# Decoding 64-bit weights: the sign by an 8-bit conversion, or by a parametric ReLU and a shift

## The chip, the cores and the metric

The kernel runs on one core of a Trainium2 chip. The metric is the device time of one execution in microseconds (us). Before the change it is 1642.6 us, the median of three runs (1642.33 to 1644.14).

The core has five engines with queues of their own, and each takes its instructions strictly in the order in which they were queued: PE (TensorE: matmuls and transposes), DVE (VectorE), ACT (ScalarE), POOL (GpSimd) and SP (SyncE, which here only issues DMAs). An instruction that waits holds up everything behind it on its engine, and nothing on the others until they need its result.

## The reference

Two blocks follow each other: an attention that keeps the 32 largest scores of each row, and a two-layer network with an ELU between the layers.

```python
# q, k, v: (8, 8, 576, 64) float32
scores = scale * np.matmul(q, k.transpose(0, 1, 3, 2))
kth = np.partition(scores, -32, axis=-1)[..., -32:-31]
scores = np.where(scores >= kth, scores, -1e9)
attn = softmax(scores)                        # with + 1e-9 in the denominator
x = np.matmul(attn, v)                        # -> (4608, 512), float32

# w_in (512, 2048), w_out (2048, 512): float64
h = x @ w_in
g = np.where(h > 0, h, np.exp(np.minimum(h, 0)) - 1)
out = (g @ w_out).astype(np.float32)
```

What matters here is that the two weight matrices arrive as float64. No engine computes in that type, so the kernel makes float32 words out of the 64-bit words itself. That is the *decoding*.

## The kernel before, in words

**Attention.** There are 144 *steps*. A step handles one tile of query rows and one pair of heads: two *rows* of 128 x 576 scores. For each row DVE runs four `MAX8` and three `MATCH_REPLACE8` (lines 350, 354 and 360 in the first eight steps, 373, 378 and 385 after them) to find the 32nd largest score. ACT copies the scores out of PSUM (L339), masks them (L407) and takes the exponential (L408). POOL normalises (`normalise`, L418 to L425: a chain that begins with the tile `dene` and ends with two multiplications of `sc`). PE transposes the result (L444), ACT copies it out (L445), PE multiplies it with V (L470), and ACT copies that into `xT` (L497). The masks of a step come one step or more after its `MAX8`s, and `normalise` one step after the masks.

**Network.** When the `xT` of a block of tokens is full, its matmuls go into a list: the hidden layer (L545), the ELU around it (L555 to L564 on ACT, L515 on POOL or L517 on DVE), and the projection (L573). `feed` takes pieces from this list between the passes of a step, by a budget that is reckoned when the program is written out; it is the same before and after the change.

**Decoding.** The weights are cut into 32 *pieces* of 128 x 512 numbers, 16 of `w_in` and 16 of `w_out`. Each is loaded as 128 x 1024 32-bit words (`load_weight`, L155, issued on SP) into one of eight `raw` buffers, and goes through four stages, every one on strided words (each second one):

1. `convert_first`, on POOL (L176): the high words, read as float32, are clamped. Below this is called the *clamp*.
2. `convert_second`, on ACT (L182, L183, L185): this function is what changes.
3. `convert_third`, on DVE (L189): the words that stage 2 left in the place of the low words are shifted left by 3.
4. `convert_last`, on POOL (L193): those are added as integers to the words that stage 2 left in the weight tile. Below this is called the *add*. It frees the `raw` buffer, and so lets the load of the piece eight places later be issued.

`decode_piece(i)` issues the load of piece i + 3, the clamp of piece i, stage 2 of piece i - 1, stage 3 of i - 3 and stage 4 of i - 4. `hook` calls it twice in each row of the first seven steps, and after that three times in a step. So in the order in which the program is written, the add of a piece comes right behind the clamp of the piece four later.

**Who sets the order.** From the ninth step on (`n == tight`, with `tight` = 8) the order on each engine is the written one (`manual_schedule`, L729). The first eight steps, in which most of the decoding lies, are outside it, and there the framework itself orders each engine's instructions when the program is made. The profile shows where it left the written order. When the last piece is done, the buffers of the decoding are given up, and others take their place, among them those into which the K and Q of the second batch are loaded (`load_halves`, L231).

Of the kernel before, what the change touches and what calls it, by code (L numbers as in the profile page):

```python
# [8 lines left out]
AF = mybir.ActivationFunctionType  # L9
ALU = mybir.AluOpType  # L10
FP32 = mybir.dt.float32
U32 = mybir.dt.uint32
I32 = mybir.dt.int32
FP8 = mybir.dt.float8e4
PSUM = bass.MemoryType.PSUM

TOP_K = 32
# [64 lines left out]
def kernel(  # L82
# [9 lines left out]
    nc = tc.nc  # L92
# [15 lines left out]
    scale = 1.0 / float(D) ** 0.5  # L108
# [35 lines left out]
    def weight(i):  # L144
        per = dff // WN
        if i < NC * per:
            f, c = divmod(i, NC)
            src = moe_w_in[c * P : (c + 1) * P, 2 * f * WN : 2 * (f + 1) * WN]
            return src, w_in[:, c, f * WN : (f + 1) * WN]
        f = i - NC * per  # L150
        return moe_w_out[f * P : (f + 1) * P, :], w_out[:, f, :]
# [6 lines left out]
    def parts(t):  # L158
        words = t[:].rearrange("p (n w) -> p n w", w=2)
        return words[:, :, 0], words[:, :, 1]  # L160
# [16 lines left out]

    def convert_second(i):
        lo, hi = parts(raw[i])
        ef = hi.bitcast(FP32)  # L180
        w = weight(i)[1]
        nc.scalar.activation(w, lo, AF.Copy, scale=2.0**-35, bias=2.0**17)  # L182
        nc.scalar.activation(lo.bitcast(FP32), ef, AF.Abs, scale=2.0**-112)  # L183
        signs = w.bitcast(FP8).rearrange("p (n w) -> p n w", w=4)[:, :, 3]
        nc.scalar.activation(signs, ef, AF.Copy, scale=2.0**-30, saturate=False)  # L185

    def convert_third(i):
        lo = parts(raw[i])[0]
# [22 lines left out]
    def decode_piece(i):  # L211
        if i + 3 < 2 * NF:
            load_weight(i + 3)
        apart = 1 if i >= scheduled else 0
        stages = [(0, convert_first), (1, convert_second)]
        if i != scheduled:
            stages += [(3 + apart, convert_third), (4 + apart, convert_last)]
        for ago, stage in stages:
            if 0 <= i - ago < 2 * NF:
                stage(i - ago)  # L220
        decoded[0] = max(0, i - 3 - apart)
# [380 lines left out]
    for b in range(B):  # L602
# [28 lines left out]
        for qts in order:  # L631
# [3 lines left out]
            for qt in qts:  # L635
                n = len(steps)
# [155 lines left out]
```

## Time and profile before

| | |
|---|---|
| median of three runs | 1642.6 us (1642.33 to 1644.14) |
| span of the profiled execution, first to last instruction | 1640.8 us |
| median less this span | 1.8 us |
| busy: PE, DVE, ACT, POOL | 1581.7, 1453.4, 1187.7, 708.7 us |
| first and last instruction of the decoding | 3.1 us (load), 153.7 us (last add ends) |

The profile names an execution's span only; its time outside the span isn't shown, and the 1.8 us above stand in for it. Every number of the profile comes from one execution. "Idle before" is the time in which an engine stood still just before an instruction, and behind "<-" stands who ended that wait. A clock below 1.00 for PE ("PEclk") means that PE was granted that share of its full speed, and its matmuls take longer in proportion.

### The profile page before, as it was taken

The page shows a single profiled execution, that of the slowest core. Times are in us where ns is not written, and L with a number is a line of the kernel's source. Part 1 is how long each engine was busy: PE and PEld are TensorE (multiplying, and loading weights), DVE is VectorE, ACT ScalarE, POOL GpSimd, SP SyncE. Part 2 cuts the span into 40 slices and gives each one's busy share as a digit, 9 for nine tenths or more (in the row PEclk, how much of TensorE's full clock was granted, in tenths as well). Part 3 has the DMA queues.
Part 4 walks back from the last instruction along what each step waited for, and adds up shares of the span by engine and source line. Part 5 has one row for each costly group of instructions (what it writes and reads, how often), then busy time and mean ns, then how long its engine had stood idle before and what let it go on. Part 6 is the DMA issues. An engine that isn't in the chain of part 4 may idle for free.

```text
span 1640.8 us, 25344 instructions
## 1 busy us (share of the span) xinstructions
PE 1581.7 (96%) x8276; PEld 1011.8 (62%) x8276; DVE 1453.4 (89%) x2981; ACT 1187.7 (72%) x2400; POOL 708.7 (43%) x1534
## 2 busy tenths in 40 slices
PE   4788999999999999999999999999999999999999
PEld 3566777666575757555566666655557575755564
DVE  6987999999999999999999699999999599998000
ACT  6887778778695867778678686868759595958521
POOL 4775445445353534445335353535435353534300
PEclk8579999999999999999999999999999999999999
DMA  7431221012100310012100211012100201000000
GB/s 226 151 128 25 50 40 26 7 22 45 42 1 7 59 42 8 7 22 44 36 14 15 43 30 28 1 28 44 36 14 0 43 1 35 1 13 2 7 13 14
DMA packets 188037, 56.18 MB, mean 34 GB/s; under 512 B 178177, under 2 KB 179201, under 8 KB 187905
## 3 DMA queue, kind: packets, MB, share of 16 engines
q1 hardware_dynamic: 186704, 54.26, 14.1%
q8 instruction: 66, 1.08, 0.3%
q14 instruction: 67, 0.54, 0.1%
q10 hardware_dynamic: 1200, 0.30, 0.1%
HBM read 45.09 MB, written 9.44 MB: 33 GB/s over the span
## 4 chain that ended last, share of the span: by engine, by line
PE 76%; ACT 12%; DVE 7%; POOL 3%; issue 1%; DMA 1%; SPq 0%; ACTq 0%; DVEq 0%; POOLq 0%
PE ops L573 29%; PE hps L545 23%; PE avps L470 10%; PE scps L331 7%; PE eps L444 6%; DVE wk L378 3%; DVE m L385 3%; ACT sc L408 2%; ACT et L445 2%; ACT sc L407 2%; DVE m L373 1%; ACT n L564 1%; ACT n L555 1%; ACT sc L339 1%; ACT n L560 1%
## 5 line engine op out<-in xcount | busy, mean ns | idle before, releaser
L385 DVE MAX8 m<-wk 128x8 f32<-128x576 f32 x816 | 577.9, 752 | 0.3 <-POOL den L406 0.3
L545 PE MATMUL hps<-xT,w_in 128*128 128x256 f32 (+2 forms) x2432 | 545.8, 374 | 0.0
L573 PE MATMUL ops<-w_out,gT 128*128 128x512 f32 x1152 | 523.6, 599 | 0.0
L545 PEld LDWEIGHTS hps<-xT,w_in 128*128 128x128 f32 x2432 | 406.0, 192 | 100.1 <-issue 26.3
L378 DVE MATCH_REPLACE8 wk<-m,wk 128x576 f32<-128x576 f32 x544 | 401.4, 748 | 0.0
L573 PEld LDWEIGHTS ops<-w_out,gT 128*128 128x128 f32 x1152 | 209.0, 190 | 233.9 <-issue 232.8
L418 POOL TENSOR_SCALAR dene<-den 128x2 f32<-128x2 f32 x144 | 32.9, 228 | 686.5 <-ACT sc L408 686.1
L408 ACT ACTIVATE sc<-sc,den 128x576 f32<-128x576 f32 x288 | 223.6, 776 | 65.5 <-POOL den L406 44.2
L407 ACT ACTIVATE sc<-sc,m 128x576 f32<-128x576 f32 x288 | 225.3, 782 | 10.8 <-DVE m L385 10.7
L470 PE MATMUL avps<-et,vT 128*64 128x256 f32 (+2 forms) x2080 | 207.2, 330 | 17.4 <-ACT et L445 17.2
L425 POOL TENSOR_SCALAR sc<-sc,rec 128x576 f32<-128x576 f32 x288 | 213.0, 750 | 15.0 <-POOL rec L423 0.2
L331 PE MATMUL scps<-kqT 64*128 64x288 f32 (+1 forms) x1280 | 206.0, 442 | 13.6 <-ACT kqT L307 9.1
L339 ACT ACTIVATE sc<-scps 128x576 f32<-128x576 f32 x288 | 171.8, 647 | 65.1 <-PE scps L331 65.1
L445 ACT COPY et<-eps 128x512 f32<-128x512 f32 x288 | 164.6, 571 | 73.4 <-PE eps L444 73.4
L378 DVE MATCH_REPLACE8 wk<-m,sc 128x576 f32<-128x576 f32 x272 | 200.6, 748 | 0.0
L373 DVE MAX8 m<-sc 128x8 f32<-128x576 f32 x272 | 191.6, 749 | 8.8 <-ACT sc L339 8.8
L444 PEld LDWEIGHTS eps<-ident,sc 128*128 128x128 f32 x1152 | 144.9, 144 | 87.2 <-issue 52.7
L444 PE MATMUL eps<-ident,sc 128*128 128x128 f32 x1152 | 177.1, 279 | 13.7 <-POOL sc L425 13.7
L470 PEld LDWEIGHTS avps<-et,vT 128*64 128x64 f32 x2080 | 128.5, 142 | 98.8 <-ACT et L445 31.7
L515 POOL TENSOR_TENSOR gT<-n,gT 128x512 f32<-128x512 f32 (+1 forms) x119 | 164.9, 1386 | 31.2 <-ACT n L564 31.1
L331 PEld LDWEIGHTS scps<-kqT 64*128 64x128 f32 (+1 forms) x1280 | 111.3, 182 | 89.5 <-issue 43.8
L555 ACT ACTIVATE n<-hps 128x512 f32<-128x512 f32 (+1 forms) x156 | 87.3, 559 | 56.8 <-PE hps L545 56.0
(53 smaller groups left out, 1089.6 us busy)
## 6 DMA issues: line engine op xcount, KB each, us to landing
raw<-in_moe_w_in_dram SPq DMA_DIRECT2D x16, 512.0 KB, 6.1
vT<-in_v_dram SPq DMA_DIRECT2D x64, 128.0 KB, 2.5
raw<-in_moe_w_out_dram SPq DMA_DIRECT2D x16, 512.0 KB, 3.6
out_dram<-osb SPq DMA_DIRECT2D x32, 256.0 KB, 2.1
kin<-in_k_dram SPq DMA_DIRECT2D x112, 72.0 KB, 2.5
qin<-in_q_dram SPq DMA_DIRECT2D x112, 72.0 KB, 2.6
kin<-in_k_dram SPq DMA_DIRECT2D x8, 128.0 KB, 4.5
vT<-in_v_dram SPq DMA_DIRECT2D x64, 16.0 KB, 2.2
```

The lines of the kernel that those rows point to most:

```text
L331: nc.tensor.matmul(wide[i][rows, half, 0:HS], kq[part, q0 : q0 + u.t.ql], kq[part, k0 : k0 + HS], start=True, stop=True,)
L373: nc.vector.max(found[i], cur[i])
L378: nc.vector.match_replace(wk[i], found[i], cur[i], TAKEN)
L385: nc.vector.max(found[i], cur[i])
L407: nc.scalar.activation(sc, sc, AF.Prelu, scale=-1.0, bias=low, alpha=1.0 / STEEP)
L408: nc.scalar.activation(sc, sc, AF.Exp, scale=-STEEP, bias=gap, accum_out=u.den[:, i : i + 1])
L425: nc.gpsimd.tensor_scalar(u.sc[:, i, :], u.sc[:, i, :], rec[:, i : i + 1], 1.0, ALU.mult, ALU.mult)
L444: nc.tensor.transpose(ps[:, c * P : (c + 1) * P], sc[:, c0 : c0 + P], ident[:])
L445: nc.scalar.copy(g.et[:, chunks, u.at, :], ps[:, 0 : n * P].rearrange("p (c q) -> p c q", c=n),)
L470: nc.tensor.matmul(ps[i * D : (i + 1) * D, cols], vt[:, 2 * J + i if c == J else i * J + c, :], w, start=(c == 0), stop=(c == J),)
L545: nc.tensor.matmul(blk.h[:, f % bank, :], w_in[:, i, f * P : (f + 1) * P], blk.xT[:, i, 0:n_tok], start=(i == 0), stop=(i == NC - 1),)
L573: nc.tensor.matmul(blk.o[:], blk.gT[f // NG][:, f % NG, s * P : (s + 1) * P], w_out[:, f, :], start=(f == 0), stop=(f == NF - 1),)
```

## The change

Only `convert_second` changes. Before, ACT runs three instructions for each piece. The first writes the low words, scaled, as float32 with an offset of 2^17, so that the rounded low word sits in the last bits of that number. The second takes the absolute value of the high words, scaled, and writes it over the low words. The third writes the sign of each high word as an 8-bit float into the top byte of the weight word, and by that also clears the bits that the offset had left there.

After, it runs two. The first writes the scaled low words as rounded 32-bit integers, so there is nothing to clear. The second is a parametric ReLU over the high words: positive ones are scaled by 2^-112 as before, negative ones by a further 2^32, which sets a bit that the left shift of stage 3 moves into the place of the sign, while the sign bit itself is shifted out. Clamp, shift and add are unchanged.

```diff
-FP8 = mybir.dt.float8e4
...
     def convert_second(i):
         lo, hi = parts(raw[i])
-        ef = hi.bitcast(FP32)
-        w = weight(i)[1]
-        nc.scalar.activation(w, lo, AF.Copy, scale=2.0**-35, bias=2.0**17)
-        nc.scalar.activation(lo.bitcast(FP32), ef, AF.Abs, scale=2.0**-112)
-        signs = w.bitcast(FP8).rearrange("p (n w) -> p n w", w=4)[:, :, 3]
-        nc.scalar.activation(signs, ef, AF.Copy, scale=2.0**-30, saturate=False)
+        w = weight(i)[1].bitcast(I32)
+        nc.scalar.activation(w, lo, AF.Copy, scale=2.0**-29)
+        nc.scalar.activation(
+            lo.bitcast(FP32), hi.bitcast(FP32), AF.Prelu,
+            scale=2.0**-112, alpha=2.0**32,
+        )
```

## The prediction

> **What bounds the kernel now.** I read the busy table by stage first. The decoding lies in the first 154 us, so I cut there, and at the point from which the chain that ended last runs through PE alone.
>
> ```profile
> core 0: us, PE busy (x) PEld busy (x) DVE busy (x) ACT busy (x) POOL busy (x), PEclk, DMA share, GB/s
> 0.00:47.00 47.00, 26.10 (x111) 18.00 (x112) 32.39 (x69) 32.57 (x67) 20.95 (x40) 0.84 0.77 229
> 47.00:112.00 65.00, 52.72 (x252) 38.13 (x250) 58.52 (x117) 56.31 (x116) 45.44 (x64) 0.62 0.43 130
> 112.00:162.00 50.00, 42.92 (x224) 29.55 (x226) 40.30 (x80) 41.15 (x85) 30.74 (x53) 0.83 0.17 46
> 162.00:318.00 156.00, 152.88 (x1213) 112.91 (x1210) 154.48 (x319) 121.34 (x248) 69.54 (x163) 1.00 0.17 33
> 318.00:1640.00 1322.00, 1307.12 (x6483) 813.22 (x6483) 1167.69 (x2399) 936.35 (x1887) 541.99 (x1217) 1.00 0.11 22
> ```
>
> From 162 us on, PE or DVE is full: DVE stands still for 1.5 of 156 us, later PE for 15 of 1322. Nothing of the decoding is left there and the order is the written one, so that part can only start earlier or later as a whole. Before 162 us no engine is full: PE stands still for 40 us, DVE for 31, ACT for 32. Whatever the change is worth is decided there, and then kept to the end.
>
> Second, the waits between 47 and 112 us (time in all, times, longest).
>
> ```profile
> POOL raw L176 <- DMA raw<-in_moe_w_out_dram: 14.3, 7, 2.4
> ...
> PE eps L444 <- POOL sc L425: 10.7, 4, 4.3
> ACT et L445 <- PE eps L444: 8.6, 3, 3.2
> DVE raw L189 <- ACT raw L183: 4.2, 2, 2.5
> ...
> POOL raw L176 <- DMA raw<-in_moe_w_in_dram: 2.2, 1, 2.2
> ```
>
> The largest is POOL's clamp waiting for a weight to land. PE and ACT then wait for POOL. ACT itself holds up DVE for 4.2 us only. The timeline of POOL shows one round of this.
>
> ```profile
> 77.64 1.29 POOL L193 TENSOR_TENSOR w_in<-w_in,raw 128x512 int32<-128x512 int32 x1
> ...
> 84.02 1.28 POOL L176 TENSOR_SCALAR raw<-raw 128x512 f32<-128x512 f32 x2
> 85.25 1.29 POOL L193 TENSOR_TENSOR w_in<-w_in,raw 128x512 int32<-128x512 int32 x1
> 86.49 1.29 POOL L193 TENSOR_TENSOR w_out<-w_out,raw 128x512 int32<-128x512 int32 x1
> 90.14 0.66 POOL L176 TENSOR_SCALAR raw<-raw 128x512 f32<-128x512 f32 x1 [2.36 <-DMA raw<-in_moe_w_out_dram]
> 92.37 0.66 POOL L176 TENSOR_SCALAR raw<-raw 128x512 f32<-128x512 f32 x1 [1.57 <-DMA raw<-in_moe_w_out_dram]
> 92.98 2.56 POOL L193 TENSOR_TENSOR w_out<-w_out,raw 128x512 int32<-128x512 int32 x2
> ```
>
> Counting the L193s and L176s from the start, the two at 85.25 and 86.49 are the adds of pieces 15 and 16, those at 90.14 and 92.37 the clamps of 23 and 24. Piece 24 is loaded into the buffer that add 16 frees at 87.8, lands 4.6 us later, and POOL, which takes its queue in order, has stood still meanwhile with the adds of 17 and 18 behind it. As written, add 17 comes right behind clamp 21, but the queue has it behind clamp 24. So POOL runs in a ring: two adds 2.7 us, normalising 3.5, two clamps 1.3, two adds 2.5, the load 4.6, a clamp 0.6, together 15.2; from the adds at 77.64 to those at 92.98 it is 15.3. DVE's selection with its four shifts needs 11 us a step (14 passes at 0.66 from start to start, six value loads at 0.07, four shifts at 0.33), ACT 12.5 (four pieces at 1.76 and 5.5 for the rest), POOL without the wait 11.
>
> Why are the adds late? ACT runs behind: the masks at 90 us are those of row 9, while DVE searches row 12. Stage 2 of a piece comes late by as much, so shift and add do too. Between 47 and 112 us ACT is busy for 56 of 65 us, and its costliest part there is what the change touches:
>
> ```profile
> L183 ACT ACTIVATE raw<-raw 128x512 f32<-128x512 f32 x18 | 12.3, 683 | 0.0
> L185 ACT ACTIVATE w_out<-raw 128x512 fp8e4<-128x512 f32 x9 | 7.3, 807 | 0.0
> L185 ACT ACTIVATE w_in<-raw 128x512 fp8e4<-128x512 f32 x9 | 7.1, 784 | 0.0
> ...
> L407 ACT ACTIVATE sc<-sc,m 128x576 f32<-128x576 f32 x8 | 6.3, 784 | 0.0
> ...
> L182 ACT ACTIVATE w_in<-raw 128x512 f32<-128x512 uint32 x9 | 5.8, 679 | 0.0
> ```
>
> **The change part by part.** *The sign instruction goes.* 32 times 0.787 us are 25.2 us busy; from its start to the next start it is 0.64 us, so ACT gets 20.5 us of queue back, 2.6 in a step of four pieces (12.5 becomes 10). Where does this lie on the path?
>
> Up to 47 us the chain of waits runs through ACT at 33.6 to 38.0 and 39.8 to 42.7, with three sign instructions in it: 3 x 0.64 = 1.9 us, on the path. Between 47 and 112 the ring has no ACT step in it. If POOL's queue kept its order, ACT would only wait longer, and the gain there would be nothing. But these steps lie outside the hand-written order, and the lag of the adds, seven places instead of four, comes from ACT being the fullest engine. With ACT at 10 and DVE at 11, the reason for the lag is gone, and I expect the adds one or more places earlier against the clamps. Each place is one clamp and one add, 1.9 us, by which the load starts earlier; two places cover most of the 4.6 us. The wait at stake is 14.3 + 2.2 = 16.5 us. The end can't take all of it, because DVE is not held up that much: in this stretch it stands still for 6.5 us and its shifts take 587 instead of their usual 428 ns (17 x 0.16 = 2.7). So DVE's part is between 0 and 9 us. I take 5, a little over half, since an order that is made anew seldom removes every wait.
>
> From 112 to 162 us DVE stands still for 10 us, 4.4 of them for an ELU at 121 to 126 us while ACT works off its lag without a gap, and 5.7 for one at 157 to 162 that waits for PE's hidden layer. The first goes with the lag; for the second PE is late, and its 7 us of standing still in this stretch, in front of transposes that wait for POOL and ACT, shrink with it in part. The chain there holds two sign instructions at 141 to 148 us (1.3 us). Bounds 1.3 and 10; I take 3.5.
>
> *Parametric ReLU for the absolute value.* The trace has no such instruction on strided words. Bounds: L183 itself at 0.68 us, and the ReLU of the mask (L407), at 0.78 for 576 elements with a column as bias. That makes 0 to 0.1 us each, at most 3.2 us of ACT. I take 0, as the operands are those of L183, and 0.5 on the path as the far end.
>
> *Integers for floats as output.* L182 takes 0.68 us with float output. The nearest row with another output type is L185 at 0.79, so 0 to 0.11 each, below 3.5 us on ACT; a gain is excluded, as element count and strides stay. I take 0: both outputs are four bytes wide, L185 writes single bytes.
>
> *Waits.* The shift waited for L183, second of the three, and now waits for the ReLU, which is last of two: the same position. The add waited for the sign too, but POOL stood still for it only at the first two pieces (3.2 us at 11 and 15 us, where DVE has no score to search yet), so I count nothing. POOL and SP get no new instructions; SP's loads come when the adds do, and behind them the K and Q loads of the second batch, which wait for the last add (32.6 us in the waits of SP). They move with it.
>
> One page of the Trainium skill speaks against the change. "ScalarE: Activation LUTs", in "What ACT_TABLE_LOAD costs", says that a function outside the active table set costs a reload of about 2.66 us, and its list of sets doesn't name parametric ReLU; at two reloads a piece that would be 170 us. The row decides: the whole execution shows one table load of 1.28 us, at 2.8 us, though L407 (parametric ReLU) and L408 (exponential) alternate 288 times. So no reload enters the sum.
>
> Sum: 1.9 + 5 + 3.5 = 10.4, less 0.5 for the ReLU, about 10 us. The span goes from 1640.8 to 1631; with the 1.8 us outside it, which I leave as they are, 1632.7, or 9.9 under the median of 1642.6.
>
> **The rivals.** A measurement of this kernel can tell about 0.2%, 3.3 us, from no change.
>
> *The ring stays* (0.17). POOL keeps its order, and only 1.9 + 1.3 = 3.2 us on ACT's own path go: 1639.4, just at the bound. For it: the ring holds no ACT instruction. Against it: the lag of the adds does come from ACT.
>
> *Everything closes up* (0.14). The 16.2 us in which DVE stands still between 16 and 162 us, and 4.4 of its stretched shifts (32 x 0.14), all go: up to 20 us, 1622. Against it: PE and DVE depend on each other at 112 to 162 us, where PE's clock is 0.83 and PE is 86% busy.
>
> *The new order is worse: slower* (0.19). Today one of the two loads of a round is hidden under the normalising (3.5 us) and the clamps. If the new order puts normalising elsewhere, or a clamp in front of the pair of adds that frees its buffer's successor, the second load is laid open too, about 4 us a round, in five rounds up to 20 us; I take half, 1652. It decides as soon as less than 4.6 us of other POOL work stands between an add and the clamp eight places on. For it: the order is made from expected durations, and it has already put clamps too early once. Against it: less work on ACT brings adds forward, not back.
>
> *The new instructions cost more than the old* (below 0.03): at their upper bounds 3.2 + 3.5 = 6.7 us of ACT against 20.5 saved. The profile excludes a loss by this alone.
>
> **How the numbers follow.** Forecast 1632.7 with chance 0.50; by the bounds of its terms its own range is 1626 to 1638. The ring's case is divided by the bound, and a piece of the slower case lies within it. Faster by over 0.2%: 0.50 + 0.14 + 0.02 = 0.66. Within 0.2%: 0.16. Slower: 0.18. The range from 1622 to 1649 leaves out a piece of the closing case (0.05) and the far part of the slower one (0.10).
>
> **What would show it.** Right: L185 gone; the first two lines at 0.65 to 0.75 us; one table load; between 47 and 112 us POOL's wait for weights well under 16.5 us, with the add of a piece five or six clamps behind instead of seven; DVE's first `MAX8` of the ninth step (L373) before 106 us instead of 110.4; from 162 us on the same busy times, shifted. Wrong: the wait for weights as large as before, at an end less than 5 us earlier; or a second wait for weights in each round, and a later end; or the gain at 112 us there and given back by 318, which would mean that PE, not DVE, was late.

## The result, and the profile after

| | before | after |
|---|---|---|
| median | 1642.5 us (1639.8 to 1644.1, 4 runs) | 1634.2 us (1633.5 to 1634.5, 4 runs) |
| ratio | | 0.9945, 95% interval 0.9931 to 0.9959 |
| span of the profiled execution | 1640.8 us | 1632.6 us |
| busy: ACT, DVE | 1187.7, 1453.4 us | 1168.2, 1451.1 us |

The forecast was 1632.7 us. The time came out 1.5 us above it and the span fell by 8.2 us where 10 were forecast. In the changed kernel the line numbers behind L176 are lower by one: the clamp is L175, stage 2 is L180 and L181, the shift L188, the add L192.

First the busy table by stage, cut at the same times as before (length; busy time of PE, its weight loads, DVE, ACT and POOL; granted clock, DMA share, GB/s).

```profile
0.00:47.00 47.00, 28.80 (x113) 19.36 (x113) 32.53 (x69) 29.55 (x64) 21.31 (x41) 0.85 0.79 232
47.00:112.00 65.00, 52.11 (x250) 38.70 (x251) 54.67 (x110) 50.97 (x110) 52.34 (x73) 0.67 0.46 145
112.00:162.00 50.00, 46.04 (x298) 32.69 (x299) 49.08 (x102) 36.29 (x75) 23.73 (x43) 0.96 0.18 37
162.00:318.00 156.00, 150.99 (x1174) 110.08 (x1172) 154.88 (x320) 121.61 (x250) 70.98 (x167) 1.00 0.15 29
```

From 162 us on nothing but the start has moved. Up to that point ACT is busy for 13.2 us less. DVE did *less* than before between 47 and 112 us (54.7 for 58.5 us) and is then full: 49.1 of 50 us, for 40.3 before.

Second, the groups of ACT's instructions up to 162 us. Both new lines cost what the old ones did, and there is one table load.

```profile
L181 ACT ACTIVATE raw<-raw 128x512 f32<-128x512 f32 x32 | 20.5, 678 | 0.6 <-POOL raw L175 0.2
...
L180 ACT ACTIVATE w_out<-raw 128x512 int32<-128x512 uint32 x16 | 10.3, 682 | 0.0
...
L180 ACT ACT_TABLE_LOAD x1 | 1.3, 1283 | 2.8 <-issue 2.8
```

Third, the waits between 47 and 112 us.

```profile
PE eps L443 <- POOL sc L424: 13.8, 5, 4.0
ACT et L444 <- PE eps L443: 10.4, 5, 4.1
POOL raw L175 <- DMA raw<-in_moe_w_out_dram: 9.8, 6, 3.3
DVE raw L188 <- ACT raw L181: 6.2, 6, 3.1
```

POOL's wait for weights is 9.8 us for 14.3 + 2.2 before. Fourth, POOL's timeline shows why.

```profile
64.07 0.66 POOL L175 TENSOR_SCALAR raw<-raw 128x512 f32<-128x512 f32 x1
64.69 1.29 POOL L192 TENSOR_TENSOR w_in<-w_in,raw 128x512 int32<-128x512 int32 x1
65.95 0.66 POOL L175 TENSOR_SCALAR raw<-raw 128x512 f32<-128x512 f32 x1
66.55 1.31 POOL L192 TENSOR_TENSOR w_in<-w_in,raw 128x512 int32<-128x512 int32 x1
69.62 0.66 POOL L175 TENSOR_SCALAR raw<-raw 128x512 f32<-128x512 f32 x1 [1.76 <-DMA raw<-in_moe_w_out_dram]
```

Clamp and add now alternate instead of coming in pairs, and from the tenth add on the add of a piece stands behind the clamp five or six places later (six and seven by turns before); only the 22nd still has seven. Compared instruction by instruction, ACT's queue is the one of before with the sign instructions taken out and nothing else moved. The queues of POOL, DVE, SP and PE were ordered differently.

So the forecast's picture seems to hold: the ring was loosened, and the time fell. Whether the one caused the other is what the experiments ask, since three things happened together: the sign instructions went, POOL's order changed, and so did DVE's (with a few places on SP and PE).

### The profile page after: what moved, and what is told of

Read it like the earlier page. It is cut to its first block, busy times and chain, and to the rows that moved or that the text cites. A ratio compares the mean times of both kernels' runs of the same rounds, so it can differ in the third digit from the quotient of the medians.

```text
span 1632.6 us, 25282 instructions
## 1 busy us (share of the span) xinstructions
PE 1579.2 (97%) x8276; PEld 1009.8 (62%) x8276; DVE 1451.1 (89%) x2981; ACT 1168.2 (72%) x2368; POOL 708.9 (43%) x1534
## 4 chain that ended last, share of the span: by engine, by line
PE 74%; DVE 11%; ACT 9%; POOL 3%; issue 1%; DMA 1%; SPq 0%; ACTq 0%; DVEq 0%; POOLq 0%
PE ops L572 28%; PE hps L544 23%; PE avps L469 9%; PE scps L330 7%; PE eps L443 6%; DVE wk L377 4%; DVE m L384 3%; ACT sc L407 2%; ACT sc L406 1%; ACT et L444 1%; DVE m L372 1%; DVE wk L353 1%; ACT n L563 1%; DVE m L359 1%; DMA raw<-in_moe_w_out_dram 1%
## 5 line engine op out<-in xcount | busy, mean ns | idle before, releaser
L469 PE MATMUL avps<-et,vT 128*64 128x256 f32 (+2 forms) x2080 | 204.4, 327 | 14.3 <-ACT et L444 14.1
L443 PE MATMUL eps<-ident,sc 128*128 128x128 f32 x1152 | 176.6, 279 | 13.8 <-POOL sc L424 13.8
L330 PEld LDWEIGHTS scps<-kqT 64*128 64x128 f32 (+1 forms) x1280 | 111.0, 183 | 86.4 <-issue 45.5
```

The costliest lines, as they stand in the source:

```text
L330: nc.tensor.matmul(wide[i][rows, half, 0:HS], kq[part, q0 : q0 + u.t.ql], kq[part, k0 : k0 + HS], start=True, stop=True,)
L443: nc.tensor.transpose(ps[:, c * P : (c + 1) * P], sc[:, c0 : c0 + P], ident[:])
L469: nc.tensor.matmul(ps[i * D : (i + 1) * D, cols], vt[:, 2 * J + i if c == J else i * J + c, :], w, start=(c == 0), stop=(c == J),)
```

## The experiments

All of them are variations of the two kernels in those first eight steps. For each, POOL's idle time just ahead of clamps behind 47 us was summed from its timeline ("POOL waits"), and three points in time were read from the timelines: the start of the 20th and of the 32nd add, and the end of the masks of the sixth step (ACT's last L408 of that step). All are us. A ratio is against runs of the kernel before on the same chip, so it can differ from the ratio of the medians by some 0.06%; gains are worked out from ratios below unless two medians are named.

| kernel | median us | ratio, 95% interval | POOL waits | 20th add | sixth masks | 32nd add |
|---|---|---|---|---|---|---|
| before | 1642.5 | 1 | 17.1 | 100.9 | 108.5 | 152.4 |
| int_fp8 | 1642.9 | 1.0001, 0.9989 to 1.0014 | 15.6 | 100.6 | 108.4 | 152.1 |
| b_pin7 | 1638.7 | 0.9982, 0.9969 to 0.9995 | 10.2 | 96.2 | 106.0 | 150.0 |
| b_pin6 | 1636.0 | 0.9966, 0.9954 to 0.9978 | 0 | 94.2 | 103.2 | 148.8 |
| a_ccaa | 1635.6 | 0.9956, 0.9941 to 0.9972 | 12.7 | 101.9 | 102.2 | 148.1 |
| a_old | 1634.6 | 0.9957, 0.9945 to 0.9969 | 14.9 | 100.9 | 100.4 | 146.7 |
| after | 1634.2 | 0.9945, 0.9931 to 0.9959 | 9.8 | 93.1 | 101.5 | 147.0 |
| a_pin6 | 1632.9 | 0.9938, 0.9924 to 0.9952 | 0.5 | 88.8 | 96.8 | 143.4 |
| a_pin5 | 1632.8 | 0.9941, 0.9929 to 0.9954 | 0 | 88.2 | 96.7 | 143.4 |
| b_written | 1651.6 | 1.0061, 1.0049 to 1.0073 | 0 | 104.1 | 112.9 | 163.4 |
| a_written | 1640.3 | 0.9993, 0.9984 to 1.0003 | 0 | 96.2 | 101.2 | 153.2 |

The kernels whose name begins with b have the three instructions of before in stage 2, those with a the two of after. Outside the written pair, the first also have DVE's order of before, the second that of after; no run has the two instructions with DVE's old order.

**int_fp8: integers as output, and nothing else.** The first instruction of before writes integers; the absolute value and the sign stay.

```diff
-        nc.scalar.activation(w, lo, AF.Copy, scale=2.0**-35, bias=2.0**17)
+        nc.scalar.activation(w.bitcast(I32), lo, AF.Copy, scale=2.0**-29)
```

> One half of the change alone: the low words as rounded integers, the sign still by the third ACT instruction; as planned, every engine's queue is the one of before. Theory (POOL's queue order and the ring of loads carry the gain): the same as before, 1640.5 to 1644.5 us, POOL's wait for weights at 47 to 112 us about 16 us. Rival 1 (the integer output itself is cheaper or dearer on ACT): the first line's mean moves by 0.05 us or more from 0.68, and the time by 2 us or more. Rival 2 (ACT's freed queue time carries the gain): also the same as before.

Measured 1642.9 us, no difference. All queues were those of before. The group of this line in its profile:

```profile
L182 ACT ACTIVATE w_out<-raw 128x512 int32<-128x512 uint32 x16 | 10.3, 680 | 0.0
```

So rounding to integers is free, as the forecast took it. The kernel also serves as a repeat of before: with the same order, POOL's wait came out at 15.6 instead of 17.1 us.

**b_pin7: before, with the ring loosened a little.** Each clamp is queued behind the add of the piece seven earlier. Nothing is taken from ACT, and the queues of PE, DVE and ACT are those of before.

```diff
-        nc.gpsimd.tensor_scalar(ef, ef, top, -top, ALU.min, ALU.max)
+        clamp = nc.gpsimd.tensor_scalar(ef, ef, top, -top, ALU.min, ALU.max)
+        if i - 7 in adds:
+            tc.add_manual_dep(clamp.ins, adds[i - 7].name, ...)
...
-        nc.gpsimd.tensor_tensor(w, w, parts(t)[0].bitcast(I32), ALU.add)
+        adds[i] = nc.gpsimd.tensor_tensor(...).ins
```

> The kernel before with all its ACT work, but on POOL each clamp is queued behind the add of the piece seven places earlier, so that adds and clamps alternate as they do after the change; the queues of PE, DVE, ACT and SP are those of before. Theory (POOL's order carries the gain): most of it appears without the change, 1634 to 1638 us, with POOL's wait for weights at 47 to 112 us near 10 us. Rival (ACT's freed queue time carries it): 1641 to 1644 us.

Measured 1638.7 us: 3 us of gain, between the two expectations.

**a_ccaa: after, with POOL's pairs brought back.** From the tenth add on, POOL takes two clamps and then two adds, the add of each odd piece behind the clamp seven places on. For that `decode_piece` also writes adds and loads in pairs, which moves a few places in SP's queue.

```diff
+        if 9 <= i <= 22:
+            tc.add_manual_dep(add, made[i + 7 if i % 2 else 1 - i].name, ...)
...
```

> The changed kernel with two ACT instructions a piece, but on POOL two clamps and two adds by turns, with the adds six and seven clamps behind as before the change; the queues of PE, DVE and ACT are those of after. Theory (POOL's order): most of the gain goes, 1638 to 1643 us, with a wait for weights of 13 to 18 us at 47 to 112 us. Rival (ACT's freed queue time): 1632 to 1636 us.

Measured 1635.6 us, although POOL's wait is back at 12.7 us. That went against the order of clamps and adds as the cause.

**a_pin6: after, with the ring loosened fully.** The edit of b_pin7 with six in the place of seven, on the changed kernel.

> The changed kernel, with each clamp queued behind the add of the piece six places earlier, so that the adds are one place nearer than after; only POOL's queue differs from after. Theory (POOL's order): the rest of the wait for weights, 9.8 us at 47 to 112 us, falls below 4 us, and the time to 1627 to 1632 us. Rival (ACT): 1632 to 1636 us. Third case (PE or DVE is late next): the wait falls and the time stays at 1632 to 1636 us.

Measured 1632.9 us. POOL's wait for weights is gone (0.5 us), and the end moves by little: 1.3 us between these medians, 2.8 when both kernels were measured on one chip (below).

**a_old: after, with the whole sequence of clamps and adds of before.** A table gives for every add the clamp that it follows, so that POOL takes clamps and adds in the order that it had before; only the 24th add comes one clamp earlier than it did. ACT's and DVE's queues are those of after, PE's and SP's differ in a few places (`decode_piece` writes loads in pairs here too). Where normalising stands between them is left to the framework, and it put it earlier.

```diff
+LAG = {4: 2, 5: 3, 6: 3, 7: 6, 8: 6, 23: 6}
+LAG.update((j, 7 if j % 2 else 6) for j in range(9, 23))
...
+        for late in (clamps.get(i + LAG.get(i, 0)), adds.get(i - 1)):
+            if late is not None and 4 <= i <= 23:
+                tc.add_manual_dep(add, late.name, ...)
...
```

> The changed kernel with clamps and adds on POOL in exactly the sequence of before, from the fifth add to the 24th (the run with two clamps and two adds by turns kept the changed sequence up to the ninth add); DVE's and ACT's queues are those of after, and normalising stands up to two places earlier among them than before. Theory 1 as predicted (POOL's ring alone sets the pace, ACT only waits longer): 1638 to 1642 us. Theory 2 (two chains of nearly one length run side by side at 30 to 112 us, POOL's ring and ACT's queue, and each is slowed by the other): 1635 to 1639 us, with POOL's wait for weights after 47 us at 12 to 17 us. Theory 3 (ACT's freed time is all): 1633 to 1636 us.

Measured 1634.6 us. This is the run that decides about the ring. POOL's timeline in a_old:

```profile
69.72 2.54 POOL L197 TENSOR_TENSOR w_in<-w_in,raw 128x512 int32<-128x512 int32 x2
...
77.61 2.55 POOL L197 TENSOR_TENSOR w_in<-w_in,raw 128x512 int32<-128x512 int32 x2
82.72 0.65 POOL L178 TENSOR_SCALAR raw<-raw 128x512 f32<-128x512 f32 x1 [2.57 <-DMA raw<-in_moe_w_out_dram]
...
86.42 0.29 POOL L446 TENSOR_SCALAR dene<-den 128x2 f32<-128x2 f32 x1
86.79 1.28 POOL L197 TENSOR_TENSOR w_out<-w_out,raw 128x512 int32<-128x512 int32 x1
...
100.92 1.30 POOL L197 TENSOR_TENSOR w_out<-w_out,raw 128x512 int32<-128x512 int32 x1
```

And the same adds (the 12th, and the 20th at the end) in POOL's timeline of the kernel before:

```profile
69.70 2.54 POOL L193 TENSOR_TENSOR w_in<-w_in,raw 128x512 int32<-128x512 int32 x2
...
100.93 2.55 POOL L193 TENSOR_TENSOR w_out<-w_out,raw 128x512 int32<-128x512 int32 x2
```

The 12th and the 20th add start within 0.02 us of before, 31 us apart. So close an agreement is chance (int_fp8, with the queues of before, is 0.2 and 0.3 us off), but the ring does keep its pace, just as the forecast said it would if the order stayed. And yet the kernel ends 7 us earlier (ratio 0.9957). The ring isn't what sets the end. What sets it instead a_old can't say by itself: the sign instructions are gone, DVE has its new order, and normalising stands elsewhere: that of the fifth step starts at 86.42 us, ahead of the 17th add, where before it came behind the 19th, at 95.63. (The expectation above says up to two places earlier; here it is three adds and two clamps.)

What did come earlier is the end of the sixth step's masks, on ACT in the kernel before and then in a_old:

```profile
108.20 0.25 ACT L408 ACTIVATION_READ_ACCUMULATOR sc<-sc,den 128x1 f32 x1
```

```profile
100.23 0.21 ACT L436 ACTIVATION_READ_ACCUMULATOR sc<-sc,den 128x1 f32 x1
```

**b_pin6: before, with the ring loosened fully.** The edit of b_pin7 with six. PE's, DVE's and ACT's queues are those of before.

> The kernel before with all its ACT work, each clamp queued on POOL behind the add of the piece six places earlier, so that the load's latency is covered; the queues of PE, DVE and ACT are those of before. Theory 1 (the ring): wait for weights below 2 us and 1631 to 1636 us. Theory 2 (ACT's queue is the next chain): the wait goes, ACT is busy without a gap at 47 to 64 us and the time stays within 2 us of the run with seven places, 1636 to 1640 us. Theory 3 (ACT is all): 1640 to 1644 us.

Measured 1636.0 us. With all of the old work on ACT, 5.6 us can be had from POOL's order alone (ratio 0.9966).

**b_written and a_written: both kernels in the written order from the first step.** The written order begins before the loop over the steps instead of at the ninth.

```diff
+    ctx.enter_context(tc.manual_schedule(engines=engines))
...
-        if n == tight:
-            ctx.enter_context(tc.manual_schedule(engines=engines))
```

> The kernel before with the hand-written order from the first step on, for all engines; the adds then stand four clamps behind from the start and no load is on POOL's path. It is the partner of the next run: both have the same queues on PE, DVE and POOL, and on ACT the same but for the sign instruction. Its own time isn't forecast closely, 1625 to 1665 us.

> The changed kernel in the hand-written order from the first step on, partner of the run before: what differs is the third ACT instruction alone. Theory 1 (ring only): within 4 us of its partner. Theories 2 and 3 (ACT's own queue is a chain of its own): 5 to 15 us faster than its partner, with 20 us less busy time on ACT.

Measured 1651.6 and 1640.3 us. Between these two kernels the queues of PE, DVE and POOL are identical, ACT's differs by the 32 sign instructions and by the two that the change replaces, and POOL never waits for a weight behind 47 us. The sign instructions by themselves are worth 11.35 us here, with no wait in the ring and no new order. The sixth masks are 11.7 us earlier. This is the only pair in which nothing else of weight differs, but its order isn't the framework's.

**after_again, a_pin6_again and a_pin5**: the changed kernel beside the versions with a looser ring, on one chip. In a_pin5 the edit has five in the place of six.

> The changed kernel itself, measured beside the two that follow so that they can be compared on one chip. Expected 1634 us, 0.9945 of the kernel before.

> The changed kernel with each clamp queued behind the add six pieces earlier, a second time, now beside the changed kernel. If the ring of POOL and the load still costs the changed kernel something at its end: 1631 to 1633 us, 1 to 3 us under the changed kernel. If PE and DVE, full from 112 us on, take back whatever POOL gains: within 1 us of the changed kernel.

> The changed kernel with each clamp queued behind the add five pieces earlier: one place nearer. No load is then near POOL's path (with six the wait had already come down from 9.8 us to 0.5), so the ring theory expects the same time as with six, within 1.5 us. The theory of two chains expects POOL to wait for stage 2 and the shift of ACT and DVE instead, because the add stands in front of more clamps: 1 to 6 us over the kernel with six.

Measured 1635.5 us (1634.0 to 1637.7), 1632.7 (1631.1 to 1633.5) and 1632.8 (1631.9 to 1634.1), five runs each. The two versions with the looser ring are 2.6 to 2.8 us under the changed kernel, and alike. So a_pin6 beats both kernels, by a little. What may limit it then is in the busy table of a_pin6_again:

```profile
47.00:112.00 65.00, 55.59 (x273) 41.32 (x273) 59.49 (x120) 53.16 (x114) 55.58 (x78) 0.67 0.45 149
112.00:162.00 50.00, 44.42 (x293) 31.19 (x294) 47.46 (x98) 35.92 (x74) 21.99 (x38) 0.97 0.17 30
```

DVE is busy for 59.5 of 65 us and then for 47.5 of 50. That leaves 8 us in both stages for an earlier weight to fill. That DVE is the limit is read from this table; no run tried it.

**What the runs show together.** Read the table by its columns. The 20th add doesn't follow the median: a_old has it at the same time as before and is 7 us faster. The sixth masks do: sorted by them, the nine kernels above the written pair are sorted by their medians too, but for two neighbours whose times differ by 0.4 us each (before and int_fp8, after and a_old), well within their intervals. In the written pair the two differences are 11.7 and 11.35 us. So the end seems to hang on how soon the *attention* gets through its steps, not on how soon the ring brings the weights. That is read from how these kernels line up; no run moved the masks alone. The 32nd add lines up with the median just as well (same order, 10.2 us in the written pair). It comes in the part of the program where the decoding goes on three pieces to a step, so it may only follow the attention's pace; no run holds the one and moves the other.

Attention is a loop of its own: POOL normalises a step, PE transposes it, ACT copies the result and then, in the order of its queue, decodes two pieces and masks the next step, which POOL normalises. ACT's timeline in the kernel before shows one pass, from the copy to the end of the masks:

```profile
84.42 0.59 ACT L445 COPY et<-eps 128x512 f32<-128x512 f32 x1 [3.22 <-PE eps L444]
...
87.96 0.80 ACT L185 ACTIVATE w_out<-raw 128x512 fp8e4<-128x512 f32 x1
...
89.14 0.80 ACT L185 ACTIVATE w_out<-raw 128x512 fp8e4<-128x512 f32 x1
...
91.81 0.22 ACT L408 ACTIVATION_READ_ACCUMULATOR sc<-sc,den 128x1 f32 x1
```

And the same pass, instruction for instruction but for the two signs, in ACT's timeline of the changed kernel:

```profile
78.15 0.59 ACT L444 COPY et<-eps 128x512 f32<-128x512 f32 x1 [3.71 <-PE eps L443]
...
81.14 1.23 ACT L181 ACTIVATE raw<-raw 128x512 f32<-128x512 f32 x2
...
84.31 0.20 ACT L407 ACTIVATION_READ_ACCUMULATOR sc<-sc,den 128x1 f32 x1
```

It took 7.6 us (84.42 to 92.03) and takes 6.4 (78.15 to 84.51); 1.2 us is what two signs cost in the queue. The five passes to the masks of steps two to six add up to 38.8 us before and 33.8 after: 5.1 us, of the 6.9 by which the sixth masks are earlier. (The fifth of them gains nothing, 9.15 and 9.12 us; after the change ACT waits there for 1.1 us.) The loop also holds POOL's part, from the end of the masks to the start of normalising. For steps two to five together it is 13.8 us before (11.4 in int_fp8, so it varies), 13.4 after, 10.7 in a_old and 6.4 in b_pin6. There, clamps that wait for weights and adds stand in front of normalising. So after the change the loop is faster by ACT's part, as far as this shows; in a_old POOL's part is shorter as well; and b_pin6, whose passes on ACT take 38.8 us as before, has its gain from POOL's part. This is where POOL's order enters.

## Why the prediction was right, and where its reasons were not

**The number**: right; 1634.2 us lies in the range and 1.5 us from the forecast. The prices held: 0.64 us for a sign in the queue, nothing for the ReLU (678 ns for 676 to 683), nothing for integers, one table load. The page "ScalarE: Activation LUTs" of the Trainium skill ("What ACT_TABLE_LOAD costs") puts every switch to a different table set at about 2.66 us. The profile after shows one load of 1.28 us, as before, so no switch came with the ReLU. The 0.5 us set aside for the ReLU weren't needed.

**The step that failed**: "Between 47 and 112 the ring has no ACT step in it. If POOL's queue kept its order, ACT would only wait longer, and the gain there would be nothing." The first sentence is true of the ring, the second of the adds alone (the 20th in a_old: 100.92 for 100.93). But the forecast let the ring stand for everything in that stretch. The attention's loop runs beside it, has ACT in it, and can pull ahead of the weights: the masks of the sixth step came 8.0 us earlier in a_old (108.45 to 100.44). The rival that rests on the same step, *the ring stays* at 1639.4, fails with it. Its ring did stay in a_old and a_ccaa, and they take 1634.6 and 1635.6 us. How much of their gain is ACT's own stays open, as DVE's order and the place of normalising differ from before too; in the written pair, where they don't, the signs are worth 11.35 us.

**The mechanism**: it happened and wasn't needed. The adds moved from six and seven clamps behind (the forecast had seven throughout) to five or six, and POOL's wait fell from 16.5 to 9.8 us, both as told. But after and a_old differ by 0.4 us in the first measurement, and the changed kernel's ratio in the second one is a_old's (0.9957, interval 0.9944 to 0.9970). The 20th add comes 7.8 us sooner in after than in a_old, the 32nd 0.3 us later. So on the changed kernel the new order's own share can't be told from nothing; fully loosened it is worth 2.8 us more. On the old instructions nearly the same order is worth 3.0 us (b_pin7).

**The terms**, by the masks of the second, sixth and tenth step and the end. Up to 47 us: 1.9 forecast, 1.3 measured (45.5 to 44.2), not to be told from chance, as int_fp8 with the queues of before has 47.0. Up to 112 us: 5 forecast, 5.6 measured (108.45 to 101.51, less 1.3), inside its bounds. That this term fits is luck: it was reckoned from the ring's wait and came from the other loop. The two together, 6.9, are firmer (108.4 in int_fp8, 102.1 in after_again). From 112 to 162 us: 3.5 forecast, 0.6 measured (154.92 to 147.36, less 6.9; nothing between int_fp8 and after_again), below its lower bound of 1.3. This is the term that was mis-sized, by 3 us; the unneeded 0.5 for the ReLU and 0.6 us between the tenth masks and the end make up a part, so that the span missed by less than 2 us. The forecast read the idle time of DVE there as time to be won. Most of it did go, 40.3 us of work becoming 49.1; but 3.9 us of that work had been shifted out of the stretch before, where DVE's own queue was ordered anew and DVE now stands still for 10.3 us (6.5 before), 3.9 of them for the first ELU (1.9 before). The wait of 5.7 us at 157 to 162 shrank to 0.9 us without making the end that much earlier. Nor does the forecast's "own range" of 1626 to 1638 follow from its bounds: 1.9, 0 to 9 and 1.3 to 10, less 0 to 0.5, give 1622 to 1640.

**The marks**: the first `MAX8` of the ninth step was to start before 106 us and starts at 115.9, later than the 110.4 of before. The mark assumed that DVE keeps its order. It doesn't: it takes more of the earlier rows first (a search of the first eight steps still begins at 106.1 us, L349), the next step's search begins 2.3 us earlier than before (127.4 for 129.7) and the one of step 13 by 7.8 (160.8 for 168.6). The other marks held.

**The other rivals**: *everything closes up* needed POOL's wait to be the last obstacle. With that wait at 0 to 0.5 us, a_pin6 and a_pin5 stop at 1632.8 to 1632.9 (DVE, by the table above, is then nearly full); these orders don't come near 1622. *The new order is worse* did not come: POOL's wait for weights fell, though its longest is 3.3 us now (2.4 before).

One reading of the profile would have warned. The chain of waits of before runs through ACT from 68.6 to 80.4 us, four signs in it. The forecast followed that chain only up to 47 us. It isn't proof either. At 80.41 the view steps from a sign on ACT to normalising on POOL, but normalising reads no sign; the masks that it needs had ended at 76.2, and what held it was POOL's own add, which ended at 80.38. The view goes by the event that came last. So there the loop waited for the ring, and only the chain up to 76.2 us, with two signs, is a warning.

## What to carry to other kernels

When two loops share an in-order queue, ask for each of them separately what a cheaper instruction gives: that one loop keeps its pace says nothing about the other, and the end may hang on the other. Before crediting a gain to a new order, run the new instructions in the old order and the old ones in the new, and say what else moved with them. Here the first gave 7.1 us (a_old, with DVE's new order and an earlier normalising); the second gave 3.0 in about the order of after (b_pin7) and 5.6 fully loosened (b_pin6). New instructions fully loosened gave 10.2 (a_pin6), less than 7.1 and 5.6 together, so the gains overlap and neither can be read off the change as a whole. Idle time of an engine in a stretch isn't a gain to be had in it where a planner may move that engine's work across the boundary.

## What the runs showed of the hardware that was not expected

PE's granted clock between 112 and 162 us rose from 0.83 to 0.96 (0.97 in a_pin6_again), with 298 matmuls for 224 and only 3.1 us more of busy time. What raised the clock wasn't tried. POOL's wait for the same loads in the same order differed by 1.4 us between two executions (17.1 and 15.6 us, before and int_fp8) with medians 0.4 us apart.
